# The output of the soft mixture of experts, stored by 128 rows of one batch in place of two halves of 64 rows

## The chip, the cores and the metric

The kernel runs on one core of a Trainium2 chip. The metric is the time of one execution on the device, in microseconds (us); of several runs the median counts. Before the change it is 1020.92 us (three runs, 1020.52 to 1022.95).

## What is computed

The reference has three stages; the sizes are B = 8 batches, 8 heads, S = 576 positions, D = 64, so N = 4608 tokens of DM = 512.

```python
scores = scale * q_c @ k_c.T            # attention inside chunks of 64 positions
x = softmax(scores) @ v_c               # (N, 512) after the heads are put side by side
x = relu(x @ w_in) ** 2 @ w_out         # (512 -> 2048 -> 512)
logits = x @ phi                        # 32 slots: 8 experts of 4 slots
slot_input = softmax(logits, over tokens).T @ x
slot_out[e] = relu(slot_input[e] @ w1[e]) @ w2[e]
out = softmax(logits, over slots) @ slot_out      # (N, 512)
```

The change is about the last line: 4608 rows of 32 weights times a matrix of 32 by 512, and the way in which its result, 9.4 MB, goes to memory.

## The kernel before, in words

The tokens are worked on in NT = 36 tiles of 128. A tile holds chunk ci (64 positions) of two batches: partitions 0 to 63 are 64 rows of batch 2 bp, partitions 64 to 127 the same positions of batch 2 bp + 1. There are CPB = 9 chunks in a batch, so tile i belongs to the pair of batches bp = i // 9 and to chunk i % 9. Attention, the two large products and the soft mixture's running sums go over these tiles in blocks of three; that takes the first 930 us and is not touched.

At the end the 8 experts' weights come in as 64 units of 512 KB (w1, then w2 in two halves of DH = 256 columns), by `load_units` (L1179). Each unit takes two free places of 128 partitions by 2 KB in buffers that earlier stages have left (`freed`, L1212, puts them into the list `free`; `release`, L1611, puts a place back when the matmuls on it are recorded). All loads and all stores are issued by SP, in order, on one hardware queue.

The weights of the last softmax, `cmat` (128 tokens by 32 slots for each tile), are transposed on PE, four tiles at a time. `c_prepare` copies four tiles on POOL with each row four times over, `c_transpose` (L1240, matmuls of L1244) transposes them into a PSUM bank, and `c_parts` makes `cT` of it with ACT (L1254) and DVE or POOL (L1260): column n of tile i is token n of that tile. Four of the nine groups of four tiles (C_CHAIN) are done ahead of the experts, the others in the loop below.

Then a loop over the two halves `ch` of the columns: 16 steps of matmuls with w2 (`sop`, L1733); the result is copied (`so_sb`, L1671), spread (`s4p`, L1676) and kept in two parts (`s4`, L1678 and L1680). With `s4` of half `ch` the output of that half is made by `out_group` (L1698): for each tile one matmul of 128 by 256 columns (`ops`, L1708), two tiles to a bank of PSUM, five banks in turn; a bank is copied to an output buffer `o` by ACT (L1712) or DVE (L1710) in turn; when a group of tiles is through, two stores follow (L1718), one of partitions 0 to 63 and one of partitions 64 to 127, since the two halves lie in different batches. A group has 2 to 5 tiles of one pair of batches, in 9 groups for each half. The buffer `o` is one of three, in turn. The output of the first half of the columns is recorded between the sop steps of the second half, the output of the second half after them.

PE's order at the end is the order of the text; ACT, DVE, POOL and SP are ordered by the framework's scheduler. The framework also gives each DMA one of eight counters in turn (DMAHW0 to DMAHW7 in the rows of order), and a DMA waits until the one before it on its counter has landed.

Of the kernel before, what the change touches and what calls it, by code (L numbers as in the profile page):

```python
# [8 lines left out]
F32 = mybir.dt.float32  # L9
# [11 lines left out]
P = 128  # L21
CH = 64
# [52 lines left out]
def kernel(  # L75
# [13 lines left out]
    B, H, S, D = q.shape  # L89
# [3 lines left out]
    E, _, FE = w1.shape  # L93
    SPE = NS // E
    CPB = S // CH
    NT = B * CPB // 2
# [4 lines left out]
    dve, act, pool, pe, sp = nc.vector, nc.scalar, nc.gpsimd, nc.tensor, nc.sync  # L101
# [16 lines left out]
    big = ctx.enter_context(tc.tile_pool(name="big", bufs=1))  # L118
    sm = ctx.enter_context(tc.tile_pool(name="small", bufs=4))

    ident = const.tile([P, P], F32, name="ident")
# [52 lines left out]
    def copy(eng, out, in_, scale=None):  # L174

        if eng == "act":
            if scale is None:
                act.activation(out=out, in_=in_, func=ACTF.Copy)  # L178
            else:
                act.activation(out=out, in_=in_, func=ACTF.Copy, scale=scale)  # L180
        elif eng == "dve":
            if scale is None:
                dve.tensor_copy(out, in_)
            else:
                dve.tensor_scalar_mul(out, in_, scale)
        else:
            pool.tensor_scalar(
                out=out, in0=in_, scalar1=1.0 if scale is None else scale, scalar2=1.0,
                op0=ALU.mult, op1=ALU.mult,
            )  # L190
# [779 lines left out]
    def c_two(x):  # L970

        old, new = (range(max(0, 2 * y), min(C_CHAIN, 2 * y + 2)) for y in (x - 1, x))
        for g in old:
            c_parts(g, pool)
            if g + 2 < C_CHAIN:
                c_prepare(g + 2)
        for g in new:
            c_transpose(g, ps_h.tile([P, 512], F32, tag="h", name="cps"))
            c_todo.pop(0)
# [185 lines left out]
    DH = DM // NCH  # L1165
# [7 lines left out]
    out_tags = (f"qkv{NT % 2}", f"qkv{(NT - 1) % 2}", f"x2sb{NB % 2}")  # L1173
    kept_tags = [f"{x}{(NT - 1) % 2}" for x in ("qk16", "qkT", "qbd", "vbd")]
    kept_tags += [f"wo{f}" for f in range(4)]
    home, free = {}, []
    todo = list(units)

    def load_units():  # L1179
# [31 lines left out]

    def freed(pool_, tag, n):  # L1212
        t = pool_.tile([P, n], F32, tag=tag, name="unit", **({} if pool_ is big else {"bufs": 1}))
        free.extend((t, o, tag) for o in range(0, n // 512 * 512, 512))

    empty = set()
# [12 lines left out]
    cT, c4, c_ps = {}, {}, {}  # L1229
    c_todo = list(range(NG))  # L1230

    def c_prepare(g):
        n = min(4, NT - 4 * g)
        c4[g] = big.tile([P, 4, 4, NS], F32, tag=f"ex{g % 2}", name="c4")
        copy(
            "pool", c4[g][:, :n],
            cmat[:, 4 * g : 4 * g + n].unsqueeze(2).to_broadcast([P, n, 4, NS]),
        )

    def c_transpose(g, ps):  # L1240
        n = min(4, NT - 4 * g)
        c_ps[g] = ps[:, : n * P]
        for j in range(n):
            pe.transpose(  # L1244
                ps[:, j * P : (j + 1) * P], c4[g][:, j].rearrange("p a s -> p (a s)"), ident
            )

    def c_parts(g, eng):
        if g % 2 == 0:
# [14 lines left out]
    def c_group(ps):  # L1264
        g = c_todo.pop(0)
        c_prepare(g)
        c_transpose(g, ps)
        c_parts(g, dve)
# [248 lines left out]
    for i in range(6, NT):  # L1517
        b, j = tile_block[i]
# [17 lines left out]
    def give(*tags):  # L1536
        for pl, tag, n in tags:
            if tag in kept_tags[: (C_CHAIN + 1) // 2]:
                empty.update({(tag, 0), (tag, 512)})
            else:  # L1540
                freed(pl, tag, n)
        load_units()
# [12 lines left out]
    for g in range(min(2, C_CHAIN)):  # L1555
        at(u0 + 2 + g, lambda g=g: c_prepare(g))
# [6 lines left out]
    t = min(0, min(slots, default=0))  # L1563
# [73 lines left out]
    def c_bank(tag):  # L1637
        return ps2.tile([P, 512], F32, tag=tag, name="cps")

    waiting = []  # L1640
    for g in range(2):
        hps_g[g] = [ps2.tile([P, 512], F32, tag=f"eh{g}{h}", name="ehps") for h in range(2)]
        for kk in range(KT):
            for hf in range(2):
                for ei in range(4):
# [4 lines left out]
                        start=(kk == 0), stop=(kk == KT - 1), tile_position=(0, 32 * ei),  # L1650
# [16 lines left out]
    s4_h = {}  # L1667
# [6 lines left out]
    def slot_parts(ch, so_sb):  # L1674
# [7 lines left out]
        )  # L1682
        s4_h[ch] = s4

    GT = 1536 // DH
    out_groups = []
    for i0 in range(0, NT, CPB):
        n = -(-CPB // -(-CPB // GT))
        out_groups += [(x, min(n, i0 + CPB - x)) for x in range(i0, i0 + CPB, n)]
    if out_groups[0][1] > 2:  # L1690

        out_groups[:1] = [(0, 2), (2, out_groups[0][1] - 2)]
    step = 512 // DH
    BANKS = sum(-(-n // step) for _, n in out_groups)
    banks = ("eh00", "eh01", "eh10", "eh11", "ht0")
    bank, group_no = [0], [0]

    def out_group(ch, x):  # L1698

        i0, n = out_groups[x]  # L1700
        o = big.tile([P, GT, DH], F32, tag=out_tags[group_no[0] % 3], name="o")
        group_no[0] += 1
        for j0 in range(0, n, step):
            m = min(step, n - j0)
            ops = ps2.tile([P, step, DH], F32, tag=banks[bank[0] % 5], name="ops")
            for j in range(m):
                i = i0 + j0 + j
                pe.matmul(ops[:, j], cT[i // 8][:, i % 8], s4_h[ch], start=True, stop=True)  # L1708
            if bank[0] % 2:
                dve.tensor_copy(o[:, j0 : j0 + m], ops[:, :m])  # L1710
            else:
                act.activation(out=o[:, j0 : j0 + m], in_=ops[:, :m], func=ACTF.Copy)  # L1712
            bank[0] += 1
            yield
        bp, ci = divmod(i0, CPB)
        for c in range(2):
            r0 = (2 * bp + c) * S + ci * CH
            sp.dma_start(  # L1718
                out=out[r0 : r0 + n * CH, ch * DH : (ch + 1) * DH].rearrange(
                    "(t p) d -> p t d", p=CH  # L1720
                ),
                in_=o[64 * c : 64 * c + 64, :n],
            )

    pending, outs = None, []
    for ch in range(NCH):
        sop = ps2.tile([P, DH], F32, tag=f"so{ch % 2}", name="sop")
        for x in range(2 * FT):
            g, ft = divmod(x, FT)
            kk, t = divmod(ft, RT)  # L1730
            for ei in range(4):
                u = (1, ch, 4 * g + ei, kk)
                pe.matmul(  # L1733
                    sop[32 * ei : 32 * ei + 32], hT_g[g][:, ft, 32 * ei : 32 * ei + 32],
                    part_of(u, t // (RT // 2))[:, t % (RT // 2) * DH : (t % (RT // 2) + 1) * DH],
                    start=(x == 0), stop=(x == 2 * FT - 1),
                    tile_position=(0, 32 * ei), skip_group_check=True,
                )
            if (t + 1) % (RT // 2) == 0:
                for ei in range(4):  # L1740
                    release((1, ch, 4 * g + ei, kk), t // (RT // 2))
                load_units()
            if waiting and x == 1:
                hidden_T(*waiting.pop())
            if pending and x == 0:
                slot_parts(*pending)
                outs = [out_group(ch - 1, y) for y in range(len(out_groups))]
                pending = None
                n_out = 0

            if outs and c_todo and x > 1 and x % 2:
                c_group(c_bank("ht1"))
            while outs and n_out < (x - 2) * BANKS // (2 * FT - 3):
                n_out += 1
                while outs and next(outs[0], StopIteration) is StopIteration:
                    outs.pop(0)
# [5 lines left out]
    for y in range(len(out_groups)):  # L1762
        for _ in out_group(NCH - 1, y):
            pass
# [30 lines left out]
```

## Time and profile before

| what | value |
| --- | --- |
| median of three runs | 1020.92 us (1020.52 to 1022.95) |
| the profiled execution, its time | 1021.96 us |
| its span, first to last instruction | 1020.1 us |
| PE busy in the span | 949.6 us (93%) |
| DVE, ACT, POOL busy | 660.8, 545.3, 260.7 us |
| moved by DMA | 117.70 MB |
| of it written to memory | 9.44 MB |
| mean granted clock of PE | 0.976 |

The time is some 2 us longer than the span: the profile does not see what lies around the instructions. PE's busy share is an average over stages with different limits, and says nothing on the stage that the change touches, the last 50 us; these are read from the views of that stretch. A row of the timeline has the start, the duration, the engine (SPq is SP's issuing of a DMA), the line, and the tile that is written and those that are read.

### The profile page before, as it was taken

How to read it: one execution, taken by the hardware profiler on the slowest of the kernel's cores; microseconds unless marked ns; L12 is line 12 of the kernel's file. 1: busy time of each engine (PE TensorE's matmuls, PEld its weight loads, DVE VectorE, ACT ScalarE, POOL GpSimd, SP SyncE). 2: the span in 40 equal slices, each digit the busy share in tenths (PEclk: the TensorE clock that was granted, in tenths of full speed). 3: DMA queues.
4: the chain of work that ended last, by engine and by line, in shares of the span. 5: the costliest groups of instructions: out<-in, count | busy, mean ns of one | idle time of the engine just before them, and what ended most of it. 6: DMA issues, size and time to landing. Idle time of an engine off the chain costs nothing.

```text
span 1020.1 us, 18895 instructions
## 1 busy us (share of the span) xinstructions
PE 949.6 (93%) x7277; PEld 573.7 (56%) x7277; DVE 660.8 (65%) x1397; ACT 545.3 (53%) x1024; POOL 260.7 (26%) x265
## 2 busy tenths in 40 slices
PE   6778999899999999999999999999999999998983
PEld 5566666677666655555555555555555455554442
DVE  4998958666688876677676686776776732423142
ACT  4677664355567654565565564645555544535132
POOL 3587544422124431112111111111121110002000
PEclk9799999999999999999999999999999999999986
DMA  6767232425333543353364353353443931657988
GB/s 159 228 172 197 80 110 52 73 63 95 82 63 63 143 105 63 63 90 75 62 123 75 72 98 62 63 94 63 93 79 57 182 108 32 186 155 237 308 255 232
DMA packets 270795, 117.70 MB, mean 115 GB/s; under 512 B 230256, under 2 KB 264048, under 8 KB 270704
## 3 DMA queue, kind: packets, MB, share of 16 engines
q1 hardware_dynamic: 270704, 116.49, 48.7%
q8 instruction: 57, 0.93, 0.4%
q14 instruction: 34, 0.28, 0.1%
HBM read 78.71 MB, written 9.44 MB: 86 GB/s over the span
## 4 chain that ended last, share of the span: by engine, by line
PE 68%; DVE 15%; DMA 7%; SPq 3%; issue 2%; ACT 2%; POOL 2%; DVEq 0%; POOLq 0%; ACTq 0%
PE hps L764 28%; PE x L825 10%; PE x L827 10%; PE x L826 9%; DMA out_dram<-o 2%; PE ehps L1647 2%; DVE qk L293 2%; DMA qkv<-in_k_dram 1%; DVE stage L298 1%; PE sop L1733 1%; DVE gl L807 1%; DMA qkv<-in_v_dram 1%; SPq L377 1%; DVE qk L292 1%; DMA qkT<-qk 1%
## 5 line engine op out<-in xcount | busy, mean ns | idle before, releaser
L764 PE MATMUL hps<-xb,wi 128*128 128x384 f16 (+2 forms) x2412 | 411.3, 320 | 3.1 <-DVE wi L331 1.2
L764 PEld LDWEIGHTS <-wi 128*128 128x128 f16 x2412 | 224.5, 98 | 156.3 <-issue 14.4
L825 PE MATMUL x<-wo,gh 128*128 128x512 f16 (+1 forms) x576 | 229.8, 399 | 3.0 <-DVE x2sb L891 3.0
L826 PE MATMUL x<-wo,gh 128*128 128x512 f16 (+1 forms) x576 | 222.9, 387 | 0.0
L827 PE MATMUL x<-wo,gl 128*128 128x512 f16 (+1 forms) x576 | 207.5, 391 | 6.7 <-DVE gl L807 3.5
L807 DVE TENSOR_TENSOR gl<-g,gh 128x384 f16<-128x384 f32 (+1 forms) x162 | 95.1, 591 | 96.4 <-ACT gh L178 95.8
L788 ACT ACTIVATE g<-hps,act_w 128x384 f32<-128x384 f32 x128 | 73.7, 576 | 153.8 <-PE hps L764 133.7
L178 ACT ACTIVATE gh<-g 128x384 f16<-128x384 f32 (+3 forms) x196 | 99.8, 509 | 21.7 <-PE x L826 17.4
L484 POOL TENSOR_TENSOR ex<-ex,rs 128x512 f32<-128x512 f32 x29 | 31.2, 1075 | 289.0 <-DVE rs L481 152.4
L795 ACT ACTIVATE g<-g 128x384 f32<-128x384 f32 (+2 forms) x196 | 99.7, 509 | 5.1
L172 DVE TENSOR_REDUCE am<-qkv 128x1 bf16<-128x512 f32 x94 | 63.9, 686 | 50.5 <-DMA qkv<-in_k_dram 23.7
L433 POOL TENSOR_SCALAR vbd<-qkv,as 64x512 f16<-64x512 f32 x58 | 52.3, 902 | 155.5 <-DVE ai L208 144.8
L827 PEld LDWEIGHTS <-gl 128*128 128x128 f16 x384 | 37.2, 98 | 46.3 <-DVE gl L807 3.4
L825 PEld LDWEIGHTS <-gh 128*128 128x128 f16 x384 | 37.6, 98 | 42.8 <-ACT g L788 5.0
L788 ACT ACTIVATE g<-hps,inv_w 128x384 f32<-128x384 f32 (+1 forms) x72 | 38.5, 534 | 40.3 <-PE hps L764 24.7
L826 PEld LDWEIGHTS <-gh 128*128 128x128 f16 x384 | 37.7, 98 | 39.5 <-issue 4.4
L438 DVE SCALAR_TENSOR_TENSOR vbd<-qkv,as,vbd 64x512 f16<-64x512 f32 x58 | 53.2, 918 | 2.6 <-POOL vbd L433 1.6
L423 DVE SCALAR_TENSOR_TENSOR qk<-qkv,as,qk 128x512 f16<-128x512 f32 x58 | 53.7, 936 | 0.9 <-ACT qk L418 0.5
L448 DVE COPY qbd<-qkT 64x1024 f16<-64x1024 f16 x58 | 25.6, 441 | 41.6 <-DMA qkT<-qk 41.2
L807 POOL TENSOR_TENSOR gl<-g,gh 128x384 fp32r<-128x384 f32 (+2 forms) x39 | 42.1, 1081 | 37.4 <-ACT gh L178 29.1
L827 PEld LDWEIGHTS x<-wo,gl 128*128 128x128 f32 x192 | 35.8, 190 | 15.5 <-POOL gl L807 4.9
L474 ACT ACTIVATE ex<-ex,es 128x512 f32<-128x512 f32 x29 | 20.8, 718 | 41.4 <-DVE ex L468 41.4
(240 smaller groups left out, 1422.8 us busy)
## 6 DMA issues: line engine op xcount, KB each, us to landing
unit<-in_moe_w_dram SPq DMA_DIRECT2D x36, 512.0 KB, 4.3
unit<-in_moe_w_dram SPq DMA_DIRECT2D x56, 256.0 KB, 5.9
qkv<-in_q_dram SPq DMA_DIRECT2D x72, 128.0 KB, 3.3
qkv<-in_k_dram SPq DMA_DIRECT2D x72, 128.0 KB, 3.4
qkv<-in_v_dram SPq DMA_DIRECT2D x72, 128.0 KB, 3.4
stage<-in_moe_w_in_dram SPq DMA_DIRECT2D x16, 512.0 KB, 4.1
stage<-in_moe_w_out_dram SPq DMA_DIRECT2D x16, 512.0 KB, 5.4
out_dram<-o SPq DMA_DIRECT2D x16, 256.0 KB, 4.1
```

The lines of the kernel that those rows point to most:

```text
L172: dve.tensor_reduce(out=am, in_=src, axis=AX.X, op=ALU.max, apply_absolute_value=True)
L178: act.activation(out=out, in_=in_, func=ACTF.Copy)
L423: dve.scalar_tensor_tensor(out=qk16[:, 2 * a + 1], in0=flat[:, a], scalar=v["s"][:, a : a + 1], in1=qk16[:, 2 * a], op0=ALU.mult, op1=ALU. ...
L433: pool.tensor_scalar(out=dst[0], in0=vin, scalar1=v["s"][pr, 2:3], scalar2=1.0, op0=ALU.mult, op1=ALU.mult,)
L438: dve.scalar_tensor_tensor(out=dst[1], in0=vin, scalar=v["s"][pr, 2:3], in1=dst[0], op0=ALU.mult, op1=ALU.subtract,)
L764: pe.matmul(hp, wi[f][:, wl, kt], xb[:, xl, kt, :n], start=(nm == 0), stop=(nm == 3 * KT - 1))
L788: act.activation(out=r["g"], in_=r["hp"], func=ACTF.Relu, scale=sc)
L795: act.activation(out=g, in_=g, func=ACTF.Square)
L807: (dve if eng == "dve" else pool).tensor_tensor(out=r["gl"], in0=r["g"], in1=r["gh"] if parts16(b) else r["gh"].bitcast(F32), op=ALU.subtract,
L825: pe.matmul(o, gh[:, c], w[:, 0], start=first, stop=False)
L826: pe.matmul(o, gh[:, c], w[:, 1], start=False, stop=False)
L827: pe.matmul(o, gl[:, c], w[:, 0], start=False, stop=last)
```

## The change

It does four things.

1. Groups of tiles become groups of parts. A part (i, c) is 128 rows in a line of one batch: chunks i and i + 1 of batch c of the pair. That works for an even tile i whose neighbour i + 1 is of the same pair of batches (`in_pairs`). The four tiles that have no such neighbour, 8, 9, 26 and 27, are kept as they were ("lone") and go last, as one group. A half of the columns then has 10 groups: 2 and 2 parts, seven groups of 4 parts, and the 4 lone tiles.
2. So that a part is one matmul, `c_transpose` writes the columns of a pair's two tiles in another order: the 64 tokens of batch 0 of both, then the 64 of batch 1 of both. The output of a transpose is so two runs of 64 columns with 64 between them.
3. A group is stored by one DMA of 128 partitions (L1757) in place of two of 64; the lone group by eight DMAs of 64 rows (L1763).
4. The buffer `o` of a group is an emptied buffer of the experts' weights (1024 elements wide, both places free), taken out of the list for good, once no unit is left to load (`out_buffer`). Only if none is free is it one of the three. At the build each of the 20 groups gets one of its own, 20 different buffers.

```diff
     def c_transpose(g, ps):
...
         for j in range(n):
-            pe.transpose(
-                ps[:, j * P : (j + 1) * P], c4[g][:, j].rearrange("p a s -> p (a s)"), ident
-            )
+            i = 4 * g + j
+            dst = ps[:, j * P : (j + 1) * P]
+            if in_pairs(i):
+                dst = ps[:, j // 2 * 2 * P : (j // 2 + 1) * 2 * P].rearrange(
+                    "p (c j s) -> p j c s", c=2, j=2
+                )[:, j % 2]
+            pe.transpose(dst, c4[g][:, j].rearrange("p a s -> p (a s)"), ident)
...
-    out_groups = []
-    for i0 in range(0, NT, CPB):
-        n = -(-CPB // -(-CPB // GT))
-        out_groups += [(x, min(n, i0 + CPB - x)) for x in range(i0, i0 + CPB, n)]
...
+    out_groups, lone = [], []
+    for bp in range(NT // CPB):
+        i0 = bp * CPB
+        pairs = [i for i in range(i0, i0 + CPB) if i % 2 == 0 and in_pairs(i)]
+        lone += [(i, None) for i in range(i0, i0 + CPB) if not in_pairs(i)]
+        for c in range(2):
+            group_ = [(i, c) for i in pairs]
...
+            out_groups.append(group_)
+        if len(lone) == 4:
+            out_groups.append(lone)
+            lone = []
...
+    def out_buffer():
+
+        if not todo:
+            tags = [t for _, _, t in free]
+            for tag in tags:
+                if size_of[tag] == 1024 and tags.count(tag) == 2:
+                    free[:] = [x for x in free if x[2] != tag]
+                    return big.tile([P, 4, DH], F32, tag=tag, name="o")
+        group_no[0] += 1
+        return big.tile([P, GT, DH], F32, tag=out_tags[group_no[0] % 3], name="o")
...
-                i = i0 + j0 + j
-                pe.matmul(ops[:, j], cT[i // 8][:, i % 8], s4_h[ch], start=True, stop=True)
+                i, c = parts[j0 + j]
+                rows = cT[i // 8][:, i % 8 + (c or 0)]
+                pe.matmul(ops[:, j], rows, s4_h[ch], start=True, stop=True)
...
-        for c in range(2):
-            r0 = (2 * bp + c) * S + ci * CH
...
+        if parts[0][1] is not None:
+            r0 = at_(*parts[0])
             sp.dma_start(
...
+                out=out[r0 : r0 + n * P, cols].rearrange("(t p) d -> p t d", p=P), in_=o[:, :n]
+            )
+        else:
+            for j, c in ((j, c) for j in range(n) for c in range(2)):
+                r0 = at_(parts[j][0], c)
+                sp.dma_start(out=out[r0 : r0 + CH, cols], in_=o[CH * c : CH * c + CH, j])
```

Where the stores stand on SP, at the seam of the two halves of the columns, before (each row names what it waits for; out_0_dram is the output, o_... a group's buffer):

```order
L1718 DMA out_0_dram<-o_11273 64x5x256 [waits DMAHW2_49,DVE_49,Activation_49]
L1718 DMA out_0_dram<-o_11273 64x5x256 [waits DMAHW3_49]
L1718 DMA out_0_dram<-o_11295 64x4x256 [waits DMAHW4_49,DVE_49,Activation_49]
L1718 DMA out_0_dram<-o_11295 64x4x256 [waits DMAHW5_49]
L1718 DMA out_0_dram<-o_11313 64x2x256 [waits DMAHW6_49,Activation_49]
L1718 DMA out_0_dram<-o_11313 64x2x256 [waits DMAHW7_49]
L1718 DMA out_0_dram<-o_11320 64x3x256 [waits DMAHW0_49,DVE_49,Activation_49]
L1718 DMA out_0_dram<-o_11320 64x3x256 [waits DMAHW1_49]
```

and with the change, from the last wide store of the first half on:

```order
L1757 DMA out_0_dram<-o_11267 128x4x256 [waits DMAHW4_49,DVE_49,Activation_49]
L1763 DMA out_0_dram<-o_11285 64x256 [waits DMAHW5_49,Activation_49]
L1763 DMA out_0_dram<-o_11285 64x256 [waits DMAHW6_49]
L1763 DMA out_0_dram<-o_11285 64x256 [waits DMAHW7_49]
L1763 DMA out_0_dram<-o_11285 64x256 [waits DMAHW0_49]
L1763 DMA out_0_dram<-o_11285 64x256 [waits DMAHW1_49,DVE_49]
L1763 DMA out_0_dram<-o_11285 64x256 [waits DMAHW2_49]
L1763 DMA out_0_dram<-o_11285 64x256 [waits DMAHW3_49]
L1763 DMA out_0_dram<-o_11285 64x256 [waits DMAHW4_49]
L1757 DMA out_0_dram<-o_11309 128x2x256 [waits DMAHW5_49,Activation_49]
L1757 DMA out_0_dram<-o_11315 128x2x256 [waits DMAHW6_49,DVE_49]
```

In place of two stores a group there is one, over 128 partitions; behind the first half's seven groups of four stand eight small stores, the last of which waits for the counter of the store eight before it, the last wide one, and the second half's first store stands behind it.

The copies of the second half on ACT (ops is the bank, o_... the buffer) before, where the two counters of a row are those of the two stores that read the same buffer three groups earlier:

```order
L1712 ACTIVATE o_11313<-ops_11314 128x512 [waits DMAHW0_49,DVE_49,DMAHW1_49,PE_49,Activation_49]
L1712 ACTIVATE o_11320<-ops_11325 128x256 [waits DMAHW2_49,DVE_49,DMAHW3_49,PE_49,Activation_49]
L1712 ACTIVATE o_11330<-ops_11335 128x512 [waits DMAHW4_49,DVE_49,DMAHW5_49,PE_49,Activation_49]
L1712 ACTIVATE o_11341<-ops_11346 128x512 [waits DMAHW6_49,DMAHW7_49,PE_49,Activation_49]
L1712 ACTIVATE o_11355<-ops_11356 128x512 [waits DMAHW0_49,DVE_49,DMAHW1_49,PE_49,Activation_49]
L1712 ACTIVATE o_11366<-ops_11367 128x512 [waits DMAHW2_49,DVE_49,DMAHW3_49,PE_49,Activation_49]
```

and with the change, where the counters are those of the weights that were loaded into the buffer long ago:

```order
L1746 ACTIVATE o_11309<-ops_11310 128x512 [waits DMAHW5_49,PE_49]
L1746 ACTIVATE o_11321<-ops_11322 128x512 [waits DMAHW4_49,DMAHW0_49,PE_49]
L1746 ACTIVATE o_11331<-ops_11332 128x512 [waits DMAHW6_49,PE_49]
L1746 ACTIVATE o_11341<-ops_11342 128x512 [waits DMAHW5_49,PE_49]
L1746 ACTIVATE o_11351<-ops_11352 128x512 [waits DMAHW5_49,DMAHW3_49,PE_49]
L1746 ACTIVATE o_11361<-ops_11362 128x512 [waits DMAHW6_49,DMAHW4_49,PE_49]
```

No copy stands behind a store any more. ACT has 18 such copies in place of 20, all of 512 columns, and DVE too.

## Rows read from the trace of the kernel before

**Rows 1.** The page: the span in 40 slices, and the memory's traffic.

```profile
GB/s 159 228 172 197 80 110 52 73 63 95 82 63 63 143 105 63 63 90 75 62 123 75 72 98 62 63 94 63 93 79 57 182 108 32 186 155 237 308 255 232
...
HBM read 78.71 MB, written 9.44 MB: 86 GB/s over the span
```

**Rows 2.** The waits, 955 us to the end: engine and line, releaser, us in all, times, longest.

```profile
DVE o L1710 <- DMA out_dram<-o: 18.9, 9, 4.4
ACT o L1712 <- DMA out_dram<-o: 16.9, 10, 2.8
...
PE cps L1244 <- DVE cT L1260: 3.0, 1, 3.0
```

**Rows 3.** The chain of waits from 930 us on: start, us, what.

```profile
970.96 0.59 PE cps L1244 x4
...
971.78 0.57 PE sop L1733 x8
972.35 0.55 PE ops L1708 x3
...
976.24 4.22 DMA out_dram<-o
```

**Rows 4.** Stretches: us, busy us of PE, PEld, DVE, ACT, POOL, PE's clock, DMA share, GB/s.

```profile
962.00:970.00 8.00, 7.87 (x135) 4.46 (x138) 0.71 (x2) 1.05 (x3) 0.38 (x1) 1.00 1.10 348
982.00:983.25 1.25, 1.25 (x10) 1.03 (x12) 0.03 (x1) 0.46 (x1) 0.00 (x0) 0.50 0.00 0
983.50:984.50 1.00, 1.00 (x9) 0.38 (x2) 0.97 (x2) 0.00 (x0) 0.00 (x0) 0.50 0.95 188
985.00:988.00 3.00, 3.00 (x23) 1.44 (x22) 0.69 (x1) 1.16 (x3) 0.00 (x0) 0.62 0.92 276
994.50:996.00 1.50, 1.25 (x9) 1.12 (x9) 0.19 (x1) 0.52 (x1) 0.00 (x0) 1.00 1.02 324
1004.00:1018.00 14.00, 2.63 (x12) 1.90 (x11) 3.10 (x5) 2.66 (x5) 0.00 (x0) 0.62 0.93 255
```

**Rows 5.** Timeline of SP's issues: start, us, what.

```profile
930.25 0.37 SPq L1203 DMA_DIRECT2D unit<-in_moe_w_dram  x1
...
973.70 1.01 SPq L1208 DMA_DIRECT2D unit<-in_moe_w_dram  x1
...
974.79 41.62 SPq L1718 DMA_DIRECT2D out_dram<-o  x36
...
982.04 0.59 SPq L1718 DMA_DIRECT2D out_dram<-o  x1
```

**Rows 6.** Issues to landing: load at 973.70, all stores, store at 999.00, last store.

```profile
unit<-in_moe_w_dram SPq DMA_DIRECT2D x1, 256.0 KB, 5.6
...
out_dram<-o SPq DMA_DIRECT2D x16, 256.0 KB, 4.1
...
out_dram<-o SPq DMA_DIRECT2D x4, 128.0 KB, 4.0
...
out_dram<-o SPq DMA_DIRECT2D x1, 192.0 KB, 3.1
...
L1718 SPq DMA_DIRECT2D out_dram<-o x1: 1208/1208/1208, 1015.2 to 1015.2; - x1
out_dram<-o SPq DMA_DIRECT2D x1, 256.0 KB, 4.1
```

**Rows 7.** Timeline of PE at the end, and groups of copies there (mean ns).

```profile
992.02 0.70 PE L1676 MATMUL s4p<-so_sb,siT 128*128 128x256 f32 x2
994.75 1.89 PE L1708 MATMUL ops<-s,cT 128*128 128x256 f32 x11 [2.03 <-DVE s L1680]
...
1009.03 1.22 PE L1708 MATMUL ops<-s,cT 128*128 128x256 f32 x4 [1.74 <-DVE o L1710]
...
L1710 DVE COPY o<-ops 128x512 f32<-128x512 f32 x16 | 11.1, 692 | 22.0 <-DMA out_dram<-o 18.9 <-PE ops L1708 3.0
L1712 ACT ACTIVATE o<-ops 128x512 f32<-128x512 f32 x16 | 9.5, 597 | 20.3 <-DMA out_dram<-o 14.7 <-PE ops L1708 4.3 <-DMA unit<-in_moe_w_dram 0.6
```

More of the change, by code (lines that the diff above doesn't have):

```diff
@@ L1175 @@
     kept_tags += [f"wo{f}" for f in range(4)]
-    home, free = {}, []
+    home, free, size_of = {}, [], {}
     todo = list(units)
@@ L1213, in freed @@
         t = pool_.tile([P, n], F32, tag=tag, name="unit", **({} if pool_ is big else {"bufs": 1}))
+        size_of[tag] = n if pool_ is big else 0
         free.extend((t, o, tag) for o in range(0, n // 512 * 512, 512))
@@ L1230, with in_pairs @@
     c_todo = list(range(NG))
+    def in_pairs(i):
+        return i // 2 * 2 // CPB == (i // 2 * 2 + 1) // CPB
     def c_prepare(g):
@@ L1685 @@
     GT = 1536 // DH
-    out_groups = []
-    for i0 in range(0, NT, CPB):
-        n = -(-CPB // -(-CPB // GT))
-        out_groups += [(x, min(n, i0 + CPB - x)) for x in range(i0, i0 + CPB, n)]
-    if out_groups[0][1] > 2:
-        out_groups[:1] = [(0, 2), (2, out_groups[0][1] - 2)]
+    out_groups, lone = [], []
[5 more added lines that the diff above has]
+            group_ = [(i, c) for i in pairs]
+            if not out_groups:
+                out_groups.append(group_[:2])
+                group_ = group_[2:]
+            out_groups.append(group_)
+        if len(lone) == 4:
+            out_groups.append(lone)
+            lone = []
+    assert not lone
+    def out_buffer():
[7 more added lines that the diff above has]
+        return big.tile([P, GT, DH], F32, tag=out_tags[group_no[0] % 3], name="o")
     step = 512 // DH
-    BANKS = sum(-(-n // step) for _, n in out_groups)
+    BANKS = sum(-(-len(x) // step) for x in out_groups)
     banks = ("eh00", "eh01", "eh10", "eh11", "ht0")
@@ L1698, in out_group @@
     def out_group(ch, x):
-        i0, n = out_groups[x]
-        o = big.tile([P, GT, DH], F32, tag=out_tags[group_no[0] % 3], name="o")
-        group_no[0] += 1
+        parts = out_groups[x]
+        n = len(parts)
+        o = out_buffer()
         for j0 in range(0, n, step):
@@ L1714, in out_group, with at_ @@
             yield
-        bp, ci = divmod(i0, CPB)
-        for c in range(2):
-            r0 = (2 * bp + c) * S + ci * CH
+        def at_(i, c):
+            bp, ci = divmod(i, CPB)
+            return (2 * bp + c) * S + ci * CH
+        cols = slice(ch * DH, (ch + 1) * DH)
+        if parts[0][1] is not None:
+            r0 = at_(*parts[0])
             sp.dma_start(
[L1719 to L1722, printed above, removed]
-            )
+                out=out[r0 : r0 + n * P, cols].rearrange("(t p) d -> p t d", p=P), in_=o[:, :n]
+            )
+        else:
+            for j, c in ((j, c) for j in range(n) for c in range(2)):
+                r0 = at_(parts[j][0], c)
+                sp.dma_start(out=out[r0 : r0 + CH, cols], in_=o[CH * c : CH * c + CH, j])
     pending, outs = None, []
```

## The prediction, before the changed kernel had run

> **What bounds the kernel now.** I read the page's time slices first. The DMA engines move 232 to 308 GB/s in the last four slices, more than in any other; 9.44 MB are written in all, the whole output, and all of it here [rows 1]. So the question is what the last 45 us wait for. The waits of 955 us to the end answer it: the copies that fill the output buffers (L1710 on DVE, L1712 on ACT) wait 18.9 and 16.9 us for stores to land, which is for one of three buffers to come free, and once PE waits 3.04 us for DVE, which stood behind such a copy [rows 2]. The chain of waits says the same: from 976 us on it alternates between a store (4.2 us for the first), a copy and the issue of the next store [rows 3]. PE, DVE and ACT are not the bound at the end; in 1004 to 1018 us they are busy 2.6, 3.1 and 2.7 of 14 us, while the DMA engines are busy 0.93 of the time [rows 4].
>
> But 0.93 busy moves only 255 GB/s, where the loads of the weights, 1.10 busy, move 348 GB/s with the same runs of 1 KB [rows 4]. Busy time per 1 KB packet is share x 16 engines / rate: 1.10 x 16 x 1.024 / 348 gives 52 ns for the loads, 60 ns for these stores, and 0.95 x 16 x 1.024 / 188 = 83 ns in 983.5 to 984.5 us, just after one lower-half store (64 partitions) was issued into an empty queue [rows 4, 5]. Where stores of both halves are mixed the rate is higher: 276 GB/s in 985 to 988 and 324 GB/s in 994.5 to 996 us [rows 4]. I read this as a limit of the side that reads the 64 partitions, not of the memory that is written, since a mixed stretch of stores alone comes within 7% of the loads.
>
> The Trainium skill has a rule for this: "SBUF — State Buffer", section "Door 1: The DMA port swizzle", says that a transfer's bandwidth goes by how many of the 16 ports its partitions reach, and 64 consecutive partitions reach eight. By it one half alone gets at most half of 435 GB/s, which the trace's 188 GB/s fits; the 324 GB/s of a mixed stretch says that two halves in flight together win much of it back, so the gain here is less than the factor of two that the rule alone would give.
>
> **Removed: the waits for a buffer.** Each of the 20 groups now has a buffer of its own, so the 18.9 and 16.9 us of waiting go, and with them PE's 3.04 us. What is late next is either the supply of data or the DMA queue. Supply, first half (columns 0 to 255): from 970.96 us PE still has 12 steps of sop, 5 of cps and 36 matmuls of ops. At the full clock these are 0.57, 0.59 and 0.55 / 3 us [rows 3], in sum 6.8 + 3.0 + 6.6 = 16.4 us, so to 987.4 us (now s4p starts at 992.02 us [rows 7]). DVE has 9 copies of 0.69 and 5 of cT of about the same in that time, ACT 14 of 0.60 [rows 7]: 9.7 and 8.4 us, both under 16.4. The steps from s4p to the next ops take 2.7 us (992.02 to 994.75 us [rows 7]), so the second half's copies begin near 990.5 us and need 9 x 0.69 = 6.2 us on DVE, or 36 x 0.31 = 11 us of PE if it runs at its lower clock (four in 1.22 us [rows 7]): done by 997 to 1002 us. All this is ahead of the queue, as follows.
>
> **Moved: the stores.** The last weight load lands at 973.70 + 5.6 = 979.3 us [rows 5, 6]; it stands ahead of every store, as before, and SP still cannot issue a store before 974.8 us [rows 5]. From 979.3 us on the queue holds stores alone. Of 9.44 MB [rows 1], 16 stores of 64 KB are 1.05 MB and the wide stores (128 partitions) are 8.39 MB.
> - Wide stores. No row shows one. Bounds: the loads' 348 GB/s, their nearest kin (128 partitions, runs of 1 KB), and the stores' 255 GB/s now: 24.1 to 32.9 us. I take 24.1, since a mix of both halves already reached 324.
> - Small stores (64 partitions, 64 KB each). Between 188 GB/s (one half alone) and 276 (both mixed) [rows 4]: 5.6 to 3.8 us for all 16; I take 4.6.
> - The seam. A store waits for the store eight before it on its counter (the rows of SP's order). The last small store of the first half so waits for the last wide one, 979.3 + 12.05 = 991.4 us; it is issued by 992.0 (a narrow issue takes 0.6 us [rows 5]), then comes the second half's first store, whose first packets I expect 1.25 us later: the queue had moved nothing from 982.0 to 983.25 us, when a store had been issued at 982.04 us into an empty queue [rows 4, 5]. Until 993.6 us the small stores are still draining. So the hole is between 0 and 1.3 us; I take 0.3.
> - The end. The last small store waits for the last wide one, at 979.3 + 24.1 + 2.3 + 0.3 = 1006.0 us. 192 KB landed 3.1 us after issue in a short queue [rows 6]; 64 KB, less 128 KB at 348 GB/s, needs 2.7: it lands at 1008.7 us. From the last landing to the end of the span are now 1020.1 - (1015.2 + 4.1) = 0.8 us [rows 6], so the span ends at 1009.5 us.
>
> Sum: 1020.1 - 1009.5 = 10.6 us less. The profiled execution took 1021.96 us with its span of 1020.1; the median of the runs, 1020.92, is 1.0 below it. I take the 10.6 off the median: **1010.3 us**.
>
> **Costed at nothing.** SP issues 34 stores in place of 36; a wide issue was 0.37 us for a load and a narrow one 0.6 [rows 5], at most 34 x 0.65 = 22 us of 34, under the queue's drain; without that cover it would be the end's 8 x 0.65 = 5.2 us, set beside the last 2 MB of wide stores (6 us). The transposes now write two runs of 64 columns in place of one of 128: between 0 and a doubling of the eight that lie on the chain before the experts, two pieces like that of 0.59 us [rows 3], so up to 1.2 us; the runs stay long, I take 0. The two fewer copies on each of ACT and DVE are hidden by the queue. The changed order of cT's columns leaves the number of matmuls, 36 a half, as it was.
>
> **The rivals.**
> - Rate in between (chance 0.10): wide stores keep the 276 GB/s of a mixed stretch. 8.39 / 0.276 = 30.4 us, 6.3 more: 1016.6 us. Against it stands 324.
> - No gain of rate (0.05): all stores stay at 255 GB/s, a limit of writing: 9.44 / 0.255 = 37.0 us in place of 28.7, 8.3 more: 1018.6 us, which is within 0.3% (3.1 us, about what a measurement can tell here) of now. Only holes like that of 982 us would be won.
> - PE slows (0.08): its granted clock is 0.50 in 982 to 983.25 us (the lower of its two levels, 1.2 GHz), after the 3.04 us wait, and 0.62 in 985 to 988 [rows 2, 4]. If it falls to that level without the wait, the second half of the loop takes twice as long (16.4 + 8), s4p starts near 995 and the second half's stores, 14.3 us by the rates above, begin near 998.5, 5 us late against 993.6: 1015 us at worst, 1012 if it falls late.
> - Small stores exposed (0.03): if a small store could leave only when the one before it had landed, each would cost about 2.7 us in place of 0.29. The place is the end of each half, where SP stands in order. Five of the 16 eat the 10.6 us whole, six make it slower by over 0.3%, all 16 give 1010.3 + 16 x 2.4 = 1049 us. Against it: each waits for a counter set eight stores before, so for wide stores that are on their way; and the four 128 KB stores of now took 4.0 us to landing where those of 256 KB took 4.1 [rows 6], so in a filled queue a small store has no time of its own. The Trainium skill, "DMA: Bandwidth & Descriptors", section "Rules for kernel authors", says against the change that transfers under 64 KB pay mostly overhead, and the same page has 0.95 us for 64 KB; by that, an estimate from that page, the 16 would cost 15.2 us in place of 4.6 and the time would be 1020.9 us, no change. No run here shows a 64 KB store yet.
> - The change without its effect: if no emptied buffer were free, the three old ones would be used. SP's and ACT's order show new buffers for every group, so I give it nothing.
>
> **How the numbers follow.** My forecast has the rest, 0.74, and spreads over 1007.5 (small stores at 276, no hole, loads' rate a little exceeded as no load is beside them) to 1013 us (wide stores at 310). The range must take in 8 of 10 and part of the slower rates and of the slow PE: 1007.3 to 1015 us. Faster by over 0.3%: 0.74 + 0.10 + 0.08 = 0.92; within 0.3%: 0.05; slower: 0.03.
>
> **What would show it.** Right: no wait of L1744 or L1746 for out_dram; PE without the idle 3 us and s4p of the second half near 987.5 us; from 979 us to the end the DMA share near 1.0 and 330 to 350 GB/s while wide stores run, under 280 where small ones do; issue of a wide store near 0.4 to 0.5 us when the queue is short; last landing near 1008.7 us. Wrong: a rate under 300 with the queue full (a limit of writing, or of another kind); an idle queue at the seam of more than 1.5 us, or SP waiting for landings while nothing else is queued; copies waiting for PE through the second half.

## The result, and the profile after

The changed kernel takes 1010.49 us (median of 4 runs, 1008.03 to 1013.5) against 1020.72 us of the kernel before on the same chip (4 runs): a ratio of 0.9898, 95% interval 0.9861 to 0.9935. The prediction was 1010.3 us. Run again in a longer comparison (a0_again below) it took 1012.84 us (10 runs) against 1020.72 (27 runs), ratio 0.9932 (0.9908 to 0.9956).

The second ratio lies within the interval of the first, and the traces say what widens these intervals: the first s4p, with which the touched stage begins, starts anywhere between 964.75 and 973.80 us in the twelve traces of this study, and the edits below do not touch what comes ahead of it. From there on the two traces of the changed kernel agree to 0.1 us (42.1 and 42.0 us), though the stage begins 5 us later in one than in the other. I therefore read the **stage**: from the start of s4p of the first half of the columns to the end of the span, in two parts, split at s4p of the second half. Before, it is 23.2 + 28.1 = 51.3 us (968.83, 992.02 [rows 7], 1020.1; one trace); after, 17.7 + 24.4 = 42.1 us. The stage became 9.2 us shorter; the medians' 10.2 and 7.9 lie on either side of that.

The start of the stage in the kernel before, on PE's timeline (start, us, engine, line, operation):

```profile
968.83 0.70 PE L1676 MATMUL s4p<-so_sb,siT 128*128 128x256 f32 x2
```

The timeline of PE in the changed kernel, 965 us to the end:

```profile
968.55 0.70 PE L1686 MATMUL s4p<-so_sb,siT 128*128 128x256 f32 x2
...
986.26 0.70 PE L1686 MATMUL s4p<-so_sb,siT 128*128 128x256 f32 x2
987.95 5.26 PE L1742 MATMUL ops<-s,cT 128*128 128x256 f32 x36 [0.99 <-DVE s L1690]
```

s4p of the second half starts at 986.26 us where it was 992.02 [rows 7], and all 36 matmuls of the second half's output run in one piece, where before they came in groups of four up to 1009 us, each behind a buffer [rows 7].

The waits of 955 us to the end (engine and line, releaser, us, times, longest):

```profile
DVE o L1744 <- PE ops L1742: 5.2, 7, 1.0
...
ACT o L1746 <- PE ops L1742: 3.8, 6, 1.1
```

The 18.9 and 16.9 us for a store [rows 2] are gone. The copies now wait for PE, which is their supply, and no copy has a row with out_dram. These waits lie in the first half of the columns and before the first copies of the second; in 989 to 993 us both engines copy without a pause (4.00 us busy of 4.00 in the stretches below).

SP's issues in the last 25 us (start, us in all, count; the last two rows are single issues, the last wide store's and the first small one's behind it), and below them answers on issue to landing (KB, us): the last wide store of the first half, the first small store behind it, the first store of the second half, its last wide store, the last two small ones:

```profile
985.90 0.37 SPq L1757 DMA_DIRECT2D out_dram<-o  x1
986.77 5.29 SPq L1763 DMA_DIRECT2D out_dram<-o  x8
992.16 8.91 SPq L1757 DMA_DIRECT2D out_dram<-o  x9
1001.16 7.09 SPq L1763 DMA_DIRECT2D out_dram<-o  x8
...
999.80 1.26 SPq L1757 DMA_DIRECT2D out_dram<-o  x1
...
1001.16 1.31 SPq L1763 DMA_DIRECT2D out_dram<-o  x1
```

```profile
out_dram<-o SPq DMA_DIRECT2D x1, 512.0 KB, 4.8
...
out_dram<-o SPq DMA_DIRECT2D x1, 64.0 KB, 4.1
...
out_dram<-o SPq DMA_DIRECT2D x1, 256.0 KB, 2.4
...
out_dram<-o SPq DMA_DIRECT2D x1, 512.0 KB, 6.5
...
out_dram<-o SPq DMA_DIRECT2D x2, 64.0 KB, 2.1
```

The last wide store of the first half so lands at 985.90 + 4.8 = 990.7 us, the first store of the second half at 992.16 + 2.4 = 994.5 us, and between them lie eight small stores that SP needs 5.29 us to issue, 0.66 us each. The same eight at the end take 7.09 us; the last is issued at 1007.65 us and lands 2.06 us later, at 1009.71; the span ends at 1010.7. The last wide store had landed at 1006.33 (999.80 + 6.53), and the last three small ones were issued only after that.

Stretches of the changed kernel (us, busy us of PE, PEld, DVE, ACT, POOL, PE's clock, DMA share, GB/s): wide stores of the first half, the seam, wide stores of the second half, the end:

```profile
979.95:984.00 4.05, 4.05 (x40) 2.30 (x39) 2.57 (x5) 1.95 (x4) 0.00 (x0) 1.00 1.08 382
984.00:988.50 4.50, 3.51 (x29) 2.00 (x29) 2.47 (x4) 1.91 (x5) 0.00 (x0) 1.00 1.03 356
989.00:993.00 4.00, 4.00 (x30) 3.64 (x28) 4.00 (x8) 4.00 (x8) 0.00 (x0) 1.00 0.51 137
993.50:996.50 3.00, 0.00 (x0) 0.00 (x0) 0.71 (x2) 0.11 (x1) 0.00 (x0) 1.00 1.06 361
996.50:1004.50 8.00, 0.00 (x0) 0.00 (x0) 0.00 (x0) 0.00 (x0) 0.00 (x0) 0.54 1.03 343
1006.00:1009.50 3.50, 0.00 (x0) 0.00 (x0) 0.00 (x0) 0.00 (x0) 0.00 (x0) 0.50 0.47 105
```

Where wide stores run, the DMA engines are full at 343 to 382 GB/s, against 255 at the end before [rows 4]. Where small ones run they are half idle: share 0.51 and 0.47. PE is at full clock until its work is done.

### The profile page after: what moved, and what is told of

Same layout as the page of the kernel before. It is cut to its first block, busy times and chain, and to the rows that moved or that the text cites. A ratio compares the mean times of both kernels' runs of the same rounds, so it can differ in the third digit from the quotient of the medians.

```text
span 1010.7 us, 18866 instructions
## 1 busy us (share of the span) xinstructions
PE 942.7 (93%) x7277; PEld 569.5 (56%) x7277; DVE 659.5 (65%) x1395; ACT 545.1 (54%) x1022; POOL 263.6 (26%) x265
## 4 chain that ended last, share of the span: by engine, by line
PE 64%; DVE 17%; DMA 6%; ACT 3%; issue 3%; SPq 3%; POOL 2%; DVEq 0%; POOLq 0%; ACTq 0%
PE hps L764 25%; PE x L825 9%; PE x L827 9%; PE x L826 9%; DMA qkv<-in_k_dram 3%; DVE qk L293 2%; DVE stage L298 2%; PE ehps L1657 2%; PE sop L1773 2%; DVE gl L807 1%; SPq L377 1%; DVE qk L292 1%; PE misc L1147 1%; DMA qkT<-qk 1%; DMA x2T<-x 1%
## 5 line engine op out<-in xcount | busy, mean ns | idle before, releaser
L178 ACT ACTIVATE gh<-g 128x384 f16<-128x384 f32 (+3 forms) x196 | 99.8, 509 | 20.7 <-PE x L826 16.4
L825 PEld LDWEIGHTS <-gh 128*128 128x128 f16 x384 | 37.6, 98 | 42.6 <-ACT g L788 5.0
L448 DVE COPY qbd<-qkT 64x1024 f16<-64x1024 f16 x58 | 26.6, 459 | 44.2 <-DMA qkT<-qk 43.7
L438 DVE SCALAR_TENSOR_TENSOR vbd<-qkv,as,vbd 64x512 f16<-64x512 f32 x58 | 51.3, 884 | 3.8 <-POOL vbd L433 2.8
```

The source lines that it names most:

```text
L438: dve.scalar_tensor_tensor(out=dst[1], in0=vin, scalar=v["s"][pr, 2:3], in1=dst[0], op0=ALU.mult, op1=ALU.subtract,)
L825: pe.matmul(o, gh[:, c], w[:, 0], start=first, stop=False)
```

## The experiments

My theory after this reading: two things together make the gain, the stores' rate (128 partitions) and the buffers (PE and the copies no longer wait), and what is left over is SP's issuing of small stores one behind the other. The rivals: the rate alone or the buffers alone do it; the number of stores, not their width, made the old ones slow; the small stores cost their bytes and no more. All kernels are edits of the changed one, and all stages come from their profiled execution.

| kernel | median us (runs) | ratio to before (95%) | stage us |
| --- | --- | --- | --- |
| before | 1020.72 (27) | 1 | 23.2 + 28.1 = 51.3 |
| a0_again | 1012.84 (10) | 0.9932 (0.9908 to 0.9956) | 17.7 + 24.3 = 42.0 |
| e1_narrow | 1022.12 (12) | 1.0013 (0.999 to 1.0036) | 17.7 + 33.1 = 50.8 |
| e2_three_buffers | 1018.56 (12) | 0.9989 (0.9968 to 1.0009) | 21.1 + 26.0 = 47.1 |
| e6_two_wide | 1015.32 (6) | 0.9928 (0.9907 to 0.9949) | 17.7 + 26.5 = 44.2 |
| e8_no_small | 1005.63 (4) | 0.984 (0.9818 to 0.9862) | 17.7 + 17.7 = 35.4 |
| e4_four_small | 1009.57 (6) | 0.9889 (0.9861 to 0.9917) | 17.7 + 20.6 = 38.3 |
| e3_lone_early | 1013.86 (6) | 0.9919 (0.9899 to 0.9938) | 17.7 + 24.9 = 42.6 |
| e34_early_four | 1009.55 (5) | 0.9868 (0.9846 to 0.989) | 17.7 + 21.0 = 38.7 |
| e9_two_queues | 1012.04 (6) | 0.9905 (0.9888 to 0.9922) | 17.7 + 23.7 = 41.4 |
| e94_two_queues_four | 1008.7 (5) | 0.9884 (0.9866 to 0.9903) | 17.7 + 21.5 = 39.2 |

The kernel before was run beside each lot: 1020.72 us with a0 to e4, 1022.44 with e6, e8, e3 and e34, 1020.92 with e9 and e94.

**The changed kernel again** (a0_again), without an edit:

> The changed kernel once more, for a narrower interval and as the yardstick of the runs beside it. Four executions gave 1008.0 to 1013.5 us in spans of 1006.2 to 1011.7. Both theories expect a median between 1008 and 1012 us. If the spread comes from the rate of the wide stores in the second half (345 GB/s in the profiled execution, 383 in the first half), the fast executions should show near 383 GB/s in both halves; 4.2 MB at 383 in place of 345 is 1.2 us, so that alone can't make 4.5 us.

Its stage is 42.0 us against 42.1, with s4p at 973.57 and 991.29 us, 5 us later than in the first trace. The stage repeats, its place does not. The median of 1012.84 us lies above the expected 1008 to 1012, and the second half did not run at 383 GB/s here either (342 in 1001.5 to 1009.5 us). SP's issues at the seam (the first row is the last wide store of the first half), and that store's issue to landing:

```profile
990.92 0.37 SPq L1757 DMA_DIRECT2D out_dram<-o  x1
...
991.80 5.21 SPq L1763 DMA_DIRECT2D out_dram<-o  x8
997.10 8.89 SPq L1757 DMA_DIRECT2D out_dram<-o  x9
...
out_dram<-o SPq DMA_DIRECT2D x1, 512.0 KB, 3.9
```

Counted from the first s4p, the last wide store of the first half lands 0.9 us earlier than in the first trace (at 21.24 us against 22.15), yet the second half's first store is issued at 23.53 us against 23.61. So the seam waits for SP's series of small issues, which starts 18.2 us after s4p in both, and not for the landing of the wide stores.

**Each wide store as two narrow ones** (e1_narrow): the buffers stay, the width goes.

```diff
-            sp.dma_start(
-                out=out[r0 : r0 + n * P, cols].rearrange("(t p) d -> p t d", p=P), in_=o[:, :n]
-            )
+            rows_ = out[r0 : r0 + n * P, cols].rearrange("(t c p) d -> c p t d", c=2, p=CH)
+            for c in range(2):
+                sp.dma_start(out=rows_[c], in_=o[CH * c : CH * c + CH, :n])
```

> The same groups and the same 20 buffers, but each wide store is written as two stores of 64 partitions. Theory 1 (the width sets the rate): the queue never waits for data, so this shows the rate of narrow stores in a full queue; at 255 to 324 GB/s the 8.39 MB take 26 to 33 us in place of 23, so 3 to 10 us more than the changed kernel, 1014 to 1020 us, with busy time per 1 KB packet near 55 to 60 ns in place of 46 to 48. Theory 2 (the buffers made the gain, the width little): within 1.5 us of the changed kernel.

Its stretches (columns as above), stores of the first half and of the second:

```profile
980.00:992.00 12.00, 11.01 (x92) 7.49 (x92) 8.25 (x14) 7.31 (x15) 0.00 (x0) 1.00 0.92 272
997.00:1014.00 17.00, 0.00 (x0) 0.00 (x0) 0.00 (x0) 0.00 (x0) 0.00 (x0) 0.50 0.89 247
```

With the buffers, PE needs the same 17.7 us for the first part, and all copies are done early. But the queue drains at 247 to 272 GB/s, and the gain is given back in the second part (33.1 us). The time cannot be told from the kernel before; it lies above the 1014 to 1020 us that I expected. Against the changed kernel, the stage is 8.7 us longer.

The 0.5 us of the stage that remain against the kernel before are not what the buffers are worth alone, since this kernel also has the 16 small stores, which the kernel before has not. Behind the last store of the other groups in each half, where only small ones are left, the queue runs low:

```profile
992.40:996.70 4.30, 0.98 (x8) 0.72 (x6) 1.98 (x4) 1.38 (x3) 0.00 (x0) 0.85 0.39 93
1014.40:1018.70 4.30, 0.00 (x0) 0.00 (x0) 0.00 (x0) 0.00 (x0) 0.00 (x0) 0.50 0.43 92
```

These 8.6 us move 0.80 MB, for which a queue at 260 GB/s would need 3.1 us. Some 5 us of this stage, an estimate from these rows, so go to the small stores. Buffers without the regrouping, which would show their own worth, were not run.

**The three old buffers** (e2_three_buffers): the width stays, the buffers go.

```diff
-        if not todo:
+        if False:
```

> The wide stores, but the three old buffers in turn. Theory 1 (width): a buffer's round is two copies (1.4 us), issue 0.4, start 1.0, 512 KB in 1.4, landing 0.3, some 4.5 us, and three of them carry 350 GB/s, so the end is held up by 1 to 3 us against the changed kernel: 1011 to 1014 us. Theory 2 (buffers): the waits of the copies for landings come back whole, PE waits again, 1017 to 1021 us.

The waits of the stage in this kernel:

```profile
ACT o L1746 <- DMA out_dram<-o: 13.2, 6, 4.6
DVE o L1744 <- DMA out_dram<-o: 10.8, 6, 3.3
...
PE ops L1742 <- ACT o L1746: 5.1, 3, 3.3
```

The copies wait for stores again, PE waits for the copies, and the queue is now and then empty: 263 GB/s at a DMA share of 0.83 in 997 to 1016 us, although nearly all its bytes go in wide stores. The time, 1018.56 us, is in the range expected if the buffers matter, though the copies' waits come back only in part (24.0 us against 35.8 [rows 2]). Against the changed kernel the stage is 5.0 us longer; against the kernel before it is 4.2 us shorter, again with the price of the small stores in it.

Taken back singly, width and buffers so cost 8.7 and 5.0 us, 13.7 in sum, where the whole change brought 9.2. The difference, 4.5 us, is near what the small stores cost beyond their bytes, 3.7 us (e8 below). So it is not shown that the two parts hide one another; by these numbers they nearly add up.

**Two wide stores for one** (e6_two_wide): as many stores and bytes as in e1, but each of 128 partitions, split by tiles.

```diff
-            sp.dma_start(
-                out=out[r0 : r0 + n * P, cols].rearrange("(t p) d -> p t d", p=P), in_=o[:, :n]
-            )
+            rows_ = out[r0 : r0 + n * P, cols].rearrange("(t p) d -> p t d", p=P)
+            for h in range(2):
+                th = slice(h * n // 2, (h + 1) * n // 2)
+                sp.dma_start(out=rows_[:, th], in_=o[:, th])
```

> Each wide store is split by tiles into two stores of all 128 partitions, so that their number and bytes are those of the narrow run and only the partitions differ. Counted from the first half's s4p to the end of the span the kernel before took 51.3 us, the changed kernel 42.1 (23.2 and 17.7 of it up to the second half's s4p) and the narrow run 50.8. Theory 1 (the 64 partitions make the narrow stores slow): 41.5 to 43.5 us and 46 to 48 ns of busy time per 1 KB packet. Rival (twice as many stores, or their smaller size, made the narrow run slow): 47 to 51 us.

Its stretches, first and second half:

```profile
976.00:987.00 11.00, 10.01 (x87) 6.59 (x86) 7.27 (x12) 6.32 (x13) 0.00 (x0) 1.00 0.95 317
990.00:1003.00 13.00, 0.00 (x0) 0.00 (x0) 0.40 (x1) 0.00 (x0) 0.00 (x0) 0.64 0.95 317
```

The stage, 44.2 us, is just above the first theory's 41.5 to 43.5 and far under the rival's 47 to 51: 2.1 us longer than the changed kernel's and 6.6 us shorter than e1's. Of the 8.7 us between those two, three quarters go with the partitions that a store reaches, and one quarter with the number of stores.

**No small stores** (e8_no_small). The stores of the lone group are left out, so 512 rows of the output are not written.

```diff
-            for j, c in ((j, c) for j in range(n) for c in range(2)):
+            for j, c in ():
```

> The stores of the lone tiles are left out (8 x 64 KB in each half; the 512 rows of tiles 8, 9, 26 and 27 stay unwritten), all else as in the changed kernel. Their bytes alone at 350 GB/s are 1.5 us a half, 3.0 us in all. Theory A (SP's serial issue of the small stores makes the seam and the end): the stage of 42.1 us falls by 6 to 7.5 us, to 34.5 to 36. Theory B (only their bytes count): it falls by 3 us, to 39.

The stage is 35.4 us, 6.7 less. The 1.05 MB of the 16 small stores would take 3.0 us at 348 GB/s; more than half of what they cost is not their bytes.

**Four small stores for eight** (e4_four_small): two tiles to a store, so the same bytes, partitions and runs, half the stores.

```diff
-            for j, c in ((j, c) for j in range(n) for c in range(2)):
+            for j, c in ((j, c) for j in range(0, n, 2) for c in range(2)):
                 r0 = at_(parts[j][0], c)
...
+                sp.dma_start(out=dst[k : k + CH], in_=o[CH * c : CH * c + CH, j : j + 2])
```

> The lone group by four stores of 128 KB in place of eight of 64 KB, all else as in the changed kernel. Theory A (the seam and the end are set by SP's issue of narrow stores, 0.6 us each, with no bytes behind them): four issues fewer in each half, 2.5 us less at the seam and 1.5 to 2.5 at the end, 4 to 5 us less than the changed kernel: near 1006 us. Theory B (the bytes of the small stores at the rate of 64 partitions set them): the same bytes, no change within 1 us.

SP's issues in this kernel, the seam and the end:

```profile
985.43 3.62 SPq L1757 DMA_DIRECT2D out_dram<-o  x3
989.55 2.98 SPq L1766 DMA_DIRECT2D out_dram<-o  x4
992.63 7.68 SPq L1757 DMA_DIRECT2D out_dram<-o  x8
1000.40 1.30 SPq L1766 DMA_DIRECT2D out_dram<-o  x1
1001.79 1.30 SPq L1757 DMA_DIRECT2D out_dram<-o  x1
1003.15 3.57 SPq L1766 DMA_DIRECT2D out_dram<-o  x3
```

The seam now takes SP 2.98 us in place of 5.29, and the stage is 38.3 us: 3.8 of the 6.7 us come back with the same bytes. At the seam, where SP's order is otherwise that of the changed kernel, the second half's first store is issued 3.6 us after its s4p (992.63 and 989.04) in place of 5.9, so 2.3 us go with the number of stores alone. For the end that is not shown by itself, since the scheduler has also put one small store ahead of the last wide one. With e34 and e94, this is among the fastest versions here; its stage is the shortest of those that write everything.

**The lone group earlier** (e3_lone_early): recorded ahead of the last pair of batches, so that wide stores follow the small ones.

```diff
+        if bp == 2:
+            lone.append((i0 + CPB, None))
+        if bp == 3:
+            lone = []
```

> The lone group stands before the last pair of batches, so that two wide stores (1 MB) follow its eight small ones in each half. Theory A: at the seam SP still issues eight small stores for 5 us, but with wide ones behind them whose data are there, and at the end the queue is full until the last wide store lands; 1 to 2 us less at the seam, 2 to 3 at the end: 37 to 39 us from the first s4p. Theory B: the same bytes, 42 us.

SP's issues in this kernel, the second half:

```profile
991.76 9.21 SPq L1761 DMA_DIRECT2D out_dram<-o  x9
1001.05 6.73 SPq L1767 DMA_DIRECT2D out_dram<-o  x8
1007.89 1.11 SPq L1761 DMA_DIRECT2D out_dram<-o  x2
```

It did not help: 42.6 us. I had expected the wide stores to keep the queue full over the small ones. But those ahead are issued no faster than the queue drains, and while SP issues eight small stores in 6.73 us the queue runs low (266 GB/s over 1000 to 1008 us); the two wide stores behind them leave SP only at 1007.89 us. The eight issues cost SP about the same here as at the very end (6.73 and 7.09 us).

**Both edits** (e34_early_four), the two diffs above together:

> Both: the lone group before the last pair of batches, and by four stores of 128 KB. With four small stores alone the stage took 38.3 us. Theory A: the rest of the hole at the seam and the small stores at the end go, 36.5 to 38 us and a time 1 to 2 us under that of the four small stores alone. Theory B (the seam is by now bound by PE's 17.7 us and by bytes): 38.3 us again.

38.7 us against 38.3 of e4, where 36.5 to 38 was expected if the place helped: nothing more is won by it. By medians the two cannot be told apart.

**Small stores from two engines** (e9_two_queues): in the second half, four of the eight are issued by ACT.

```diff
-                sp.dma_start(out=out[r0 : r0 + CH, cols], in_=o[CH * c : CH * c + CH, j])
+                (act if c and ch else sp).dma_start(out=out[r0 : r0 + CH, cols], in_=o[CH * c : CH * c + CH, j])
```

> The changed kernel, but in the second half of the columns four of the eight small stores (the lower tokens' partitions 64 to 127) are issued by ACT instead of SP. Bytes, partitions, packets and number of stores are unchanged. Stage = from the first s4p to the end of the span, 42.1 us in the changed kernel (17.7 + 24.4). Theory A (the eight small stores at the end cost SP's issues in series, some 0.64 us each): with two engines issuing, four of those issues run beside the other four, so the second part falls from 24.4 to 22.4 to 23.2 us, the stage to 40.1 to 40.9, the last store lands 1.2 to 2 us nearer to the last wide one's landing than the 3.4 us of the changed kernel. Theory B (what costs is a small store's own way, 64 partitions and the time from issue to landing, whoever issues it): stage 42.1 within 0.4, last landing still 3 us or more after the last wide one's. Ratio to before: A 0.988 to 0.990, B 0.990 to 0.993, too near to tell them apart; the stage tells.

SP's issues in this kernel, then ACT's:

```profile
993.76 10.72 SPq L1757 DMA_DIRECT2D out_dram<-o  x9
1004.58 4.30 SPq L1763 DMA_DIRECT2D out_dram<-o  x4
```

```profile
994.94 4.72 ACTq L1763 DMA_DIRECT2D out_dram<-o  x4
```

41.4 us, between the two theories. ACT's four leave 5 to 10 us before the first of SP's, beside the wide stores, and the last small store lands 1.0 us after the last wide one (1010.34 and 1009.38 us) in place of 3.4. But SP's nine wide issues now take 10.72 us in place of 8.91, so the last wide store lands later. From the first landing of the second half (996.13 us) to the end of the span are 15.2 us against 16.1 in the changed kernel, so 1.0 us is won of the 1.2 to 2.0 expected; 0.3 is lost at the seam, which the edit does not touch. The Trainium skill, "DMA: Bandwidth & Descriptors", section "Rules for kernel authors", says that spreading transfers over several issuing engines brings no bandwidth and saves only issue time, since all run on the same DMA engines. The trace agrees: with both engines issuing, and ACT's small stores among the bytes, 327 GB/s were moved, where the changed kernel moved 343 in the same stretch, and SP's nine wide issues became longer.

```profile
996.50:1004.50 8.00, 0.00 (x0) 0.00 (x0) 0.00 (x0) 0.00 (x0) 0.00 (x0) 0.63 1.05 327
```

**Four small stores, from two engines** (e94_two_queues_four):

> The lone group by four stores of 128 KB (stage 38.3 us = 17.7 + 20.6), and in the second half two of these four are issued by ACT. Theory A (issues in series): two fewer issues behind one another at the end, up to 1.2 us less: second part 19.4 to 20.2, stage 37.1 to 37.9. Theory B (a small store's own way): 38.3 within 0.3. Also whether this version is the fastest of all: A ratio 0.986 to 0.988, B 0.988 to 0.989.

39.2 us, 0.9 longer than e4 where at most 0.3 was expected, with the same ratio (0.9884 and 0.9889). In one profiled execution SP's issues among the full queue took up to 1.96 us. So a second issuing engine brings nothing beside a halved number of stores; whether it loses something is not settled by one trace.

## Why the prediction was right

**The bound.** The end was bound by the buffers together with the stores' rate, as read from the waits [rows 2] and the stretches [rows 4]. e1 and e2 show that both are needed for the 9.2 us: without the width no copy waits for a store, but the queue drains at 247 GB/s and is the bound; without the buffers the waits remain. What each would bring without the small stores was not run.

**PE.** Predicted: 16.4 us of work from 970.96, s4p at 987.4. Measured 986.26, on an execution whose first s4p starts 0.3 us earlier: within 0.9 us, without an idle piece. The rival in which PE slows did not come: the clock is 1.00 in every stretch in which PE works.

**The rate.** The step that carried the most weight, wide stores at the loads' 348 GB/s, held: 382 and 356 in the first half, 361 and 343 in the second. The rivals with 276 and 255 GB/s fall. e6 against e1 supports the reason given, the side that reads 64 partitions. The Trainium skill, "DMA: Bandwidth & Descriptors", section "Rules for kernel authors", advises one transfer of 128 partitions in place of two of disjoint halves. e1 and the changed kernel agree with that advice, by 8.7 us here.

**The seam.** First packets of the second half were expected near 993.3 us; the rate rises from 137 GB/s to 361 between 993.0 and 993.5. The moment was right by luck, for the path was another. The prediction let the last small store wait for the landing of the last wide one, at 991.4 us. That store landed at 990.70, and the last small one was issued at 991.46, 0.04 us after the issue before it had ended; in a0_again it came 1.6 us after the landing (996.41 and 994.81).

**The small stores: the term that was mis-sized.** The prediction gave them 2.3 us at the seam, 0.3 for the hole and 2.7 at the end, in sum 5.3. Left out (e8), they give back 6.7. That 1.4 is the whole shortfall: the stage was predicted at 1009.5 - 968.8 = 40.7 us, and is 42.1; without the small stores it comes to 35.4 both as predicted (40.7 - 5.3) and as measured. The step that failed stands under "Costed at nothing": SP's issues "under the queue's drain", the last eight beside 2 MB of wide stores, so that the last small store of a half was timed by the landing of the last wide one. The runs show SP's serial issues in that place.

At the end SP did not get far enough ahead. Where it issues stores one behind the other under the full queue, an issue lasts 1.2 to 1.4 us in place of 0.37 for a wide and 0.59 for a small store (999.80 and 1001.16 us above), so it stays near the queue's own pace. The last wide store leaves SP at 1001 us, only 5.3 us before it lands; two small issues pass in 1.3 to 1.4 us, a third in 1.1, and the other five follow some 0.64 us apart while the queue runs empty (share 0.47 from 1006.0 us on). That issue and not bytes or partitions is the bound is shown at the seam, by e4 (2.3 us back with half the stores) and by a0_again (the same issue time with an earlier landing). At the end it is read from SP's rows and supported by e4 and e9, which change other things with it.

The rival of exposed small stores had the right place, the end of each half, but another mechanism (each waiting for the landing of the one before) and a price of 2.7 us a store; the eight at the end cost 3.4 us beyond the last wide landing. The 0.95 us that the prediction took from the Trainium skill ("DMA: Bandwidth & Descriptors") stands there, in section "Bandwidth", for 64 KB loaded over 128 partitions by a DMA that GpSimd issues, which is another case. By it the 16 would cost 15.2 us, an estimate; measured are 6.7, 0.42 each.

**The transposes.** Costed at nothing, they cost nothing that shows: four on PE take 0.66 us before (at 970.89 us) and after (970.61).

**The predicted time.** 1010.3 agreed with the first median to 0.2 us, more closely than the terms did: the stage gave 9.2 us, not 10.6, and the place of the stage in an execution makes up the rest. That closeness is luck; the second median, 1012.84, lies 2.5 us off, still within the range.

## What to carry to other kernels

Read the rate of the queue while it is full before pricing the removal of a wait for it. Price each part of a change against the kernel that has all the rest: here that gives 8.7 us for the width and 5.0 for the buffers. Against the kernel before, the same two runs show 0.5 and 4.2, because both also carry the small stores that the regrouping brought. Store with all 128 partitions, and count the issues of small stores one by one on their engine, at the measured 0.6 us each, where they come last or between two phases: of the last eight here, three were issued after the last wide store had landed.

## What the runs showed that I had not expected

- SP's issue of a wide store stretches: 0.37 us at 985.90, 1.26 at 999.80 us. In the first half, where a copy came before each issue, it stayed at 0.37 though the stores took 4.7 to 6.5 us to land there too; in the second half, issued one behind the other, it became 1.2 to 1.3 us from the sixth store on. I read this as the reason why e3 failed: SP could not put the stores far ahead of the queue. What sets the limit, bytes outstanding or the pace of issues, was not tried.
- With a short queue a wide issue takes 0.37 us, a narrow one 0.59, whatever its bytes: the store of 64 KB costs SP more time than the one of 512 KB.
- The full queue moved 382 and then 356 GB/s in the first half, 361 and then 343 in the second, with stores of the same form. Small stores are not the reason: e8, which has none, shows 377 in 980 to 984 us and 341 in 993.5 to 1001. Why it falls stays open; so does the difference of the narrow stores, 272 against 247 GB/s.
- The beginning of the last stage moves by 9 us from one execution to another, so the ratios of one kernel in two comparisons differ by 0.3%, while its stage came out at 42.1 and 42.0 us.
